# Batch 0 folded in two load halves, third-stage angles first among the tables, first-stage copies shared with the vector engine, and the products of an accumulating bank moved: a Fourier-mixing plus MLP-mixer kernel

## Chip, cores, metric

The kernel runs on one core of one Trainium2 chip. The metric is device time in microseconds (us); the 36 runs of the kernel before that are on record lie between 602.35 and 606.16. Engines in the profile: PE is the matrix engine (PEld its weight loads), DVE the vector engine, ACT the scalar engine, POOL (GpSimd) the general one, which also asks for most loads here.

## The reference, cut to what matters

```python
X = np.fft.fft(np.fft.fft(x, axis=1), axis=2).real       # x: 8 x 3008 x 256, float32
h = np.maximum(X.transpose(0, 2, 1) @ w_tok1, 0) @ w_tok2          # tokens, width 256
u = X + h.transpose(0, 2, 1)
out = u + np.maximum(u @ w_ch1, 0) @ w_ch2                         # channels, width 1536
```

The kernel computes in 16-bit floats and takes the Fourier transforms as products with tables of cosines and sines, which it makes itself while the first batch loads.

## The kernel before, where the change and the argument touch it

A batch goes through a *front*: its token rows are loaded twice (`xp` forwards, `xm` by a gather of backward rows with indices `ix8`), folded into even and odd parts `eo` and `pad`, multiplied by the first-stage table (`z`), then by the feature table `td` (`w`), then by the third-stage tables `tp` and `tq` (`yt`); the token MLP follows (`uu`, `ut`). Then come six *chunks* of channel MLP per batch: `pc` is the first layer, `pa` and `pb` hold the second. For most chunks the second layer uses seven products instead of eight, with sums `s` of the activations and weight sums `t1w` to `t4w`. The front of a later batch is woven into the chunks of the one before; the front of batch 0 stands alone at the start, where nothing can hide it.

The loads and the first tables (`ts`, `tt` and `stt` issue to DVE unless `eng=G`; `act` to ACT; `gdma` and `gather` are asked for by GpSimd):

```python
    new_x(0)
    load_xp(0)                                   # whole rows of batch 0
    iota(kb[:]...); iota(krow[:]...); iota(jrow[:]...)     # GpSimd
    ...
    ts(rowi[:], rowi[:], -2.0, AT.mult)
    ts(ix8[:], ix8f[:], rowi[:], AT.add, 0.0, AT.max)      # 128 x 16, one SBUF input
    load_xm(0, 0)
    load_xm(0, 1)
    ...
    load_w1p(); load_w1m()                       # first token weights, turned by tables
    ...                                          # later:
    def load_rest():
        load_wc1(0)                              # first channel weights, first half
        ...                                      # w2n, second token weights
        load_wc1(1)                              # first channel weights, second half
        gdma(wc2[:, :, 0:D], ...)                # second channel weights
```

The fold, the turns of the third-stage table, and the first stage (generators; each `yield` is a place where the caller may put other work between):

```python
        for t0, t1 in ((9, 17), (1, 9)) if b == 0 else ...:      # in fold(b, eng)
            tt(fa[:], xp[:, t, 1:128], rv[:, :, 255:128:-1], AT.add, eng)   # rv: rows of xm
            yield
            tt(fb[:], rv[:, :, 1:128], xp[:, t, 255:128:-1], AT.add, eng)
            ...
    def back(k, sgn):                            # turned tables for the token weights
        for c in range(3):
            ...
            nc.tensor.matmul(pr[:], lhsT=anti[:], rhs=tts[k][:, c4], start=True, stop=True)
            if k:
                act(tts[k + 1][:, c4], pr[:], scale=sgn)         # back(2): ACT
            else:
                V.tensor_copy(out=tts[k + 1][:, c4], in_=pr[:])  # back(0): DVE
            yield
        ...
        for t0 in (11, 6, 1):                    # in front(b): first stage
            for half in range(2):
                ...                              # ten products (b == 0) into pz
                copy(half == 0 and b > 0, zo[:, :, :, t0:t0 + 5], ...)   # True: DVE, else ACT
                yield
```

The order of batch 0's front, and the placing of the seven products in the chunks:

```python
    filler(12)                                   # products without use: keep the clock up
    take(fold0, 5)
    ...                                          # four small operations on the table td
    take(fold0, 5)
    own = front(0)
    take(tu_q, 3); take(tu_p, 2); take(own, 2); take(tu_r, 3)
    filler(4)
    take(own, 2); take(tu_b0, 2); take(own, 4); take(tu_b0, 1)
    new_x(1); load_xp(1)                         # loads of batch 1
    for k in range(2):
        load_xm(1, k)
    for k in range(6):                           # second stage, with the token weights turned
        take(own, 2)
        take(tu_b2, 1 if 0 < k < 4 else 0)
        take(car, 1)
    ...
    sum_at = {0: 1, 1: 2, 3: 4, 4: 3}            # column tile: sum s to make
    places = {0: 0, 1: -1, 2: 1, 4: 2, 6: 3, 7: 4, 9: 5, 11: 6}   # column tile: product
                # 0, 2, 4, 5 add into the bank pa; 1, 3, 6 are the bank pb; -1 only reads pa
```

After the first chunk product, GpSimd runs `weight_sums()` (two copies and four operations of about 1.5 us each) and DVE starts the fold of batch 1.

## Time and profile before

| | before |
|---|---|
| time, median of 2 | 603.07 us (602.35 to 603.78) |
| span of the profiled execution | 600.3 us |
| PE busy | 583.2 us (97%) |
| last write of `z` ends (first stage done) | 20.14 us |
| first chunk product `pc` starts | 33.92 us |
| first chunk product of batch 1 starts | 108.89 us |

PE is full nearly everywhere after 76 us, so the time is the length of PE's program plus what PE waits for. The list of waits of PE in the first 80 us of the kernel before (what was waited for, us in total, times, longest) names what is to be had:

```profile
PE filler L399 <- DVE ident L84: 8.8, 1, 8.8
PE pz L476 <- DVE eo L90: 1.0, 1, 1.0
PE pr L416 <- ACT tp L97: 0.6, 1, 0.6
PE pu L566 <- DVE ut L90: 0.4, 1, 0.4
PE pw L508 <- ACT z L97: 0.4, 1, 0.4
...
```

In the whole execution, one more line says that `pa` products waited 0.6 us for `s`. The timeline of DVE in the kernel before (start, us, line, operation, out<-in, shapes; in brackets the idle time before and who ended it):

```profile
1.87 1.72 DVE L86 TENSOR_SCALAR ix<-ix8f,rowi 128x16 int32<-128x16 f32 x1
...
10.37 0.71 DVE L90 TENSOR_TENSOR fa<-xp,xm 96x1016 f16<-96x1016 f16 x1
...
13.73 0.72 DVE L90 TENSOR_TENSOR fa<-xp,xm 96x1016 f16<-96x1016 f16 x1
...
17.88 1.29 DVE L439 CAST tts<-pr 128x512 f16<-128x512 f32 x2 [0.78 <-PE pr L435]
19.56 0.58 DVE L101 CAST z<-pz 128x96 f16<-128x96 f32 x1 [0.39 <-PE pz L476]
...
42.20 1.76 DVE L90 TENSOR_TENSOR fb<-xm,xp 96x508 f16<-96x508 f16 x1
```

Some short operations are long: 1.72 us for 16 elements, and 1.76 us for the last line. Between 16 and 20 us DVE has idle time: it makes only one of the eight copies of `z`.

The table of stretches of the kernel before (stretch, length, busy us of PE, PEld, DVE, ACT, POOL with counts, granted PE clock, DMA share, GB/s) shows the loads at about 200 GB/s from the start:

```profile
4.00:6.00 2.00, 0.00 (x0) 0.00 (x0) 1.72 (x12) 0.76 (x1) 1.52 (x3) 1.00 1.01 200
6.00:8.00 2.00, 0.00 (x0) 0.00 (x0) 1.87 (x12) 1.97 (x6) 1.92 (x4) 1.00 1.02 207
8.00:10.00 2.00, 1.20 (x12) 1.20 (x13) 1.50 (x7) 1.96 (x5) 1.92 (x5) 1.00 1.08 213
20.00:25.00 5.00, 4.75 (x49) 3.83 (x50) 3.90 (x10) 4.45 (x12) 3.32 (x5) 1.00 1.10 220
25.00:29.00 4.00, 3.93 (x44) 3.42 (x42) 3.09 (x7) 2.78 (x6) 0.96 (x1) 1.00 1.00 197
```

The clock column reads 1.00 also where no change of the clock is on record yet. The first record here is at 13.46 us, full from then on; before it the products ran at half rate (the 128-column fillers start 0.107 us apart near 9 us, products of that size 0.056 us apart after 14.3 us).

### The profile page before, as it was taken

What the parts mean: (1) busy time and instruction counts of PE and PEld (TensorE: products, weight loads), DVE (VectorE), ACT (ScalarE), POOL (GpSimd) and SP (SyncE); (2) the same over time, 40 slices, a digit from 0 to 9 for tenths busy, and PEclk for the clock granted to TensorE, in tenths of its full rate; (3) what the DMA queues carried; (4) which work ended last, traced back from release to release, by engine and by line L of the source; (5) the groups of instructions that cost most, each with busy time, mean ns of one, the idle gap of its engine ahead of it and who ended that gap; (6) DMA issues with size and microseconds to landing.
All of it is one profiled execution on the core that took longest, in us unless ns stands there. A gap on an engine that the chain in (4) does not pass through costs nothing.

```text
span 600.3 us, 15332 instructions
## 1 busy us (share of the span) xinstructions
PE 583.2 (97%) x6273; PEld 417.3 (70%) x6273; DVE 452.8 (75%) x924; ACT 387.3 (65%) x753; POOL 259.3 (43%) x396
## 2 busy tenths in 40 slices
PE   3899999999999999999999999999999999999997
PEld 3756676677767776667767777667767777666775
DVE  8779879686898668765898678856689757866663
ACT  8854665477647866577656866568665776546662
POOL 8650555937565554527348354565555100000000
PEclk9999999999999999999999999999999999999999
DMA  8993912275138914393335942278123422233533
GB/s 160 209 178 71 177 40 55 65 141 121 37 72 127 143 37 68 79 180 54 72 60 119 129 87 54 67 145 115 37 55 84 93 55 55 64 74 76 94 72 88
DMA packets 83414, 55.69 MB, mean 93 GB/s; under 512 B 53778, under 2 KB 80082, under 8 KB 82578
## 3 DMA queue, kind: packets, MB, share of 16 engines
q1 hardware_dynamic: 76816, 36.82, 32.2%
q0 software_dynamic: 6208, 17.63, 16.3%
q8 instruction: 49, 0.80, 0.6%
q10 hardware_dynamic: 320, 0.26, 0.2%
q14 instruction: 21, 0.17, 0.1%
HBM read 35.26 MB, written 24.64 MB: 100 GB/s over the span
## 4 chain that ended last, share of the span: by engine, by line
PE 81%; DVE 1%; issue 0%; ACT 0%; DVEq 0%
PE pc L662 35%; PE pa L712 17%; PE pb L712 13%; PE pu L566 5%; PE po L775 4%; PE pt L595 3%; PE pz L471 1%; PE py L538 1%; DVE s L90 1%; PE pw L508 1%; PE pw L512 1%; DVE osb L90 0%; DVE q L90 0%; DVE ut L90 0%; ACT c L97 0%
## 5 line engine op out<-in xcount | busy, mean ns | idle before, releaser
L97 ACT ACTIVATE c<-pc 128x512 f16<-128x512 f32 (+1 forms) x553 | 312.7, 591 | 159.9 <-PE pc L662 138.8
L662 PE MATMUL pc<-ut,wc 128*128 128x512 f16 (+1 forms) x1152 | 312.4, 374 | 0.4 <-DMA wc<-in_moe_w_ch_dram 0.3
L712 PEld LDWEIGHTS <-s 128*128 128x128 f16 x1968 | 122.8, 98 | 40.1 <-DVE s L90 5.7
L662 PEld LDWEIGHTS <-wc 128*128 128x128 f16 x1152 | 98.0, 98 | 55.7 <-issue 3.0
L712 PEld LDWEIGHTS <-c 128*128 128x128 f16 x1476 | 93.1, 97 | 27.8
L90 DVE TENSOR_TENSOR s<-c 128x1536 f16<-128x1536 f16 x82 | 82.0, 1000 | 4.7 <-ACT c L97 4.7
L90 DVE TENSOR_TENSOR q<-pa,uT 128x256 f32<-128x256 f32 x123 | 52.3, 425 | 36.3 <-PE pa L712 35.8
L908 POOL COPY hold<-s 128x1 f16<-128x1 f16 x29 | 5.4, 187 | 171.5 <-DVE s L90 171.5
L90 DVE TENSOR_TENSOR osb<-pb,q 128x256 f32<-128x256 f32 x123 | 51.9, 422 | 31.1 <-PE pb L712 28.4
L90 DVE TENSOR_TENSOR ut<-pu,yt 128x512 f16<-128x512 f32 (+1 forms) x96 | 63.0, 670 | 1.6 <-PE pu L566 1.5
L90 POOL TENSOR_TENSOR eo<-sab 96x512 f16<-96x512 f16 x48 | 53.9, 1139 | 1.6
L566 PE MATMUL pu<-w2r,uu 128*128 128x512 f16 (+1 forms) x168 | 50.0, 379 | 0.0
L90 POOL TENSOR_TENSOR sab<-fa,fb 96x256 f16<-96x256 f16 (+1 forms) x72 | 46.7, 673 | 0.0
L90 DVE TENSOR_TENSOR s<-s,c 128x1536 f16<-128x1536 f16 x41 | 41.1, 1003 | 0.0
L90 DVE TENSOR_TENSOR s<-c,s 128x1536 f16<-128x1536 f16 x41 | 39.5, 964 | 0.0
L97 ACT ACTIVATE w<-pw 128x257 f16<-128x257 f32 x90 | 34.6, 384 | 6.4 <-PE pw L512 3.6
L90 DVE TENSOR_TENSOR osb<-pa,uT 128x256 f32<-128x256 f32 x41 | 17.4, 424 | 24.8 <-PE pa L712 24.7
L775 PE MATMUL po<-wc,c 128*128 128x256 f16 x288 | 35.4, 273 | 0.0
L712 PE MATMUL pa<-t2w,s 128*128 128x128 f16 x492 | 34.2, 219 | 0.5 <-DVE s L90 0.4
L712 PE MATMUL pa<-t3w,s 128*128 128x128 f16 x492 | 34.2, 219 | 0.3 <-DVE s L90 0.2
L712 PE MATMUL pb<-wc,c 128*128 128x128 f16 x492 | 34.4, 219 | 0.0
L712 PE MATMUL pa<-wc,c 128*128 128x128 f16 x492 | 34.4, 219 | 0.0
(187 smaller groups left out, 747.8 us busy)
## 6 DMA issues: line engine op xcount, KB each, us to landing
out_dram<-osb SPq DMA_DIRECT2D x83, 256.0 KB
xp<-in_x_dram POOLq DMA_DIRECT2D x14, 408.0 KB, 6.6
out_dram<-osb SPq DMA_DIRECT2D x11, 192.0 KB
uT<-ut SPq DMA_TRANSPOSE x96
w2n<-in_moe_w_tok_dram POOLq DMA_DIRECT2D x2, 752.0 KB, 9.3
w1p<-in_moe_w_tok_dram POOLq DMA_DIRECT2D x2, 384.0 KB, 8.0
wc<-in_moe_w_ch_dram POOLq DMA_DIRECT2D x1, 768.0 KB, 14.7
xp<-in_x_dram POOLq DMA_DIRECT2D x2, 272.0 KB, 6.0
```

Of the source, the lines that this page charges most:

```text
L90: eng.tensor_tensor(out=out_, in0=a, in1=b, op=op)
L97: nc.scalar.activation(out=out_, in_=in_, func=func, scale=scale, **kw)
L471: nc.tensor.matmul(out_, lhsT=rows[:, half * P:half * P + P], rhs=tab, start=True, stop=True)
L508: nc.tensor.matmul(pw[:, 0:256].rearrange("p (h d) -> p h d", h=2)[:, :, 0:65], lhsT=zg[:, 0, g], rhs=td[:, 0:130].rearrange("p (h d) -> p ...
L512: nc.tensor.matmul(pw[:, 64:322].rearrange("p (h d) -> p h d", h=2)[:, :, 0:64], lhsT=zg[:, 1, g], rhs=td[:, 130:258].rearrange("p (h d) - ...
L538: nc.tensor.matmul(py[:, P * k:P * k + P], lhsT=w[:, 4 * c + k, o:o + P], rhs=tab[:, 4 * c + k, :], start=True, stop=True)
L566: nc.tensor.matmul(pu[:, 0:64 * nk], lhsT=uu[:, th, h, :], rhs=w2[:, th, :, 8 * c:8 * c + nk], start=(th == 0), stop=(th == 1))
L595: nc.tensor.matmul(pt[:, o:o + n], lhsT=hw[:, g, c], rhs=w[:, g, w0:w0 + n], start=(g == 0), stop=(g == NG - 1))
L662: nc.tensor.matmul(pc[:, 0:n], lhsT=wc1[:, h, ct * P:(ct + 1) * P], rhs=ut[:, c, h, 0:n], start=(h == 0), stop=(h == 1))
L712: nc.tensor.matmul(dst[:, P * a:P * a + P], lhsT=left[:, k, a, :], rhs=right[:, k, :], start=(first and k + a == 0), stop=(k == NH - 1), s ...
L775: nc.tensor.matmul(po[:, o:o + D], lhsT=c1[:, ct, ks * P:ks * P + P], rhs=wc2[:, ct, 0:D], start=(ct == 0), stop=(ct == NCT - 1))
L908: G.tensor_copy(out=hold[:], in_=pbox[3][:, 0, 0, 0:1])
```

## The change

The intent: shorten the 8.8 us before PE's first work and the stage after it. The upper token rows of batch 0 (9 to 16) are asked for alone, with the gather that belongs to them, so that the first fold needs fewer bytes. `ix8` becomes an operation with two SBUF inputs. The table `tp` is to be ready ahead of all others, so its turns go first, and the rest of the tables is made between the folds. DVE takes four copies of `z` and the three of `back(2)`, and gives the three of `back(0)` to ACT. All of `back(2)` and `turn_q` change places around the second stage. Last, three of the products of the chunks move one column tile later, so that their sums are ready. The diff, cut:

```diff
-    load_xp(0)
-    iota(kb...) ; iota(krow...) ; iota(jrow...)
+    load_xp(0, 9, NR)
 ...
-    ts(ix8[:], ix8f[:], rowi[:], AT.add, 0.0, AT.max)
+    stt(ix8..., ix8f..., rowi[:], zero[:], AT.add, AT.max)
     load_xm(0, 0)
+    iota(kb...) ; iota(krow...) ; iota(jrow...) ; iota(q2...)
+    load_xp(0, 0, 9)
     load_xm(0, 1)
 ... # masks from GpSimd to DVE; ident and lrot ahead of rest(m3); t1n, t1b, td into tables()
-                act(tts[k + 1][:, c4], pr[:], scale=sgn)
+                ts(tts[k + 1][:, c4], pr[:], sgn, AT.mult)
             else:
-                V.tensor_copy(out=tts[k + 1][:, c4], in_=pr[:])
+                act(tts[k + 1][:, c4], pr[:])
 ...
-                copy(half == 0 and b > 0, zo[:, :, :, t0:t0 + 5],
+                copy(half == 0 if b else t0 < 11, zo[:, :, :, t0:t0 + 5],
 ...
-    filler(12) ; take(fold0, 5) ; <td> ; take(fold0, 5) ; take(tu_q, 3) ; take(tu_p, 2)
-    take(own, 2) ; take(tu_r, 3) ; filler(4) ; take(own, 2) ; take(tu_b0, 2)
-    take(own, 4) ; take(tu_b0, 1)
+    filler(6) ; take(tu_p, 2) ; take(fold0, 3) ; take(tab, 1) ; take(fold0, 2)
+    take(own, 2) ; take(tu_r, 3) ; take(fold0, 2) ; take(tab, 1) ; take(fold0, 2)
+    take(tu_b0, 3) ; take(own, 2) ; take(tab, 1) ; take(fold0, 1) ; take(own, 2)
+    take(tu_b2, 3) ; take(own, 2)
     new_x(1) ; <loads of batch 1>
     for k in range(6):
         take(own, 2)
-        take(tu_b2, 1 if 0 < k < 4 else 0)
         take(car, 1)
+    take(tu_q, 3)
 ...
-    places = {0: 0, 1: -1, 2: 1, 4: 2, 6: 3, 7: 4, 9: 5, 11: 6}
+    places = {0: 0, 1: -1, 2: 1, 5: 2, 6: 3, 8: 4, 10: 5, 11: 6}
```

More of the change, by code (lines that the diff above doesn't have):

```diff
@@ L120, in new_x, with load_xp @@
                       xin.tile([KR, NR - 1, D], FP16, tag="xm", name="xm"))
-    def load_xp(b):
+    def load_xp(b, t0=0, t1=NR):
         xp = x_tiles[b][0]
@@ L127, in load_xp @@
                 p0 = i * QP + q
-                gdma(xp[p0:p0 + n, :, :],
-                     dram(x_t, (b * S + 16 * i + 64 * r) * D,
-                          [[64 * D, n], [1, NR * D]]))
+                gdma(xp[p0:p0 + n, t0:t1, :],
+                     dram(x_t, (b * S + 16 * i + 64 * r + t0) * D,
+                          [[64 * D, n], [1, (t1 - t0) * D]]))
     def load_xm(b, k):
@@ L157 @@
     w1m = stage.tile([P, NG, DTOK], FP16, tag="w1m")
-    tw23, q25 = pvec("tw23"), pvec("q25")
+    tw23 = pvec("tw23")
     def load_w1p():
@@ L173, in load_w1m @@
              dram(w1_t, 44 * DTOK, [[NQ * DTOK, 64], [1, 3 * DTOK]]))
+    zero = gen.tile([P, 2 * BB], FP32, tag="zero")
+    V.memset(zero[:], 0.0)
     V.memset(tw23[:], TWO23)
-    V.memset(q25[:], 0.25)
     V.memset(offrow[:, 0:2, :], 0.25)
@@ L179 @@
     iota(pcol[:], [[0, 1]], 0, 1)
-    iota(q2[:], [[1, 2]], -64, 1)
     iota(ix8f[:], [[376, BB], [1, 2]], 374, 0)
     new_x(0)
-    load_xp(0)
-    iota(kb[:].rearrange("p (c g k) -> p c g k", c=3, g=4), [[8, 3], [1, 4], [47, 64]], 0, 0)
-    iota(krow[:].rearrange("p (c g i) -> p c g i", c=3, g=4), [[8, 3], [1, 4], [4, 2]], 0, 0)
-    iota(jrow[:], [[1, 129]], 0, 0)
+    load_xp(0, 9, NR)
     ts(xicol[:], pcol[:], float(QP), AT.is_ge)
@@ L191 @@
     ts(rowi[:], rowi[:], -2.0, AT.mult)
-    ts(ix8[:], ix8f[:], rowi[:], AT.add, 0.0, AT.max)
+    stt(ix8[:].rearrange("p b k -> p (b k)"), ix8f[:].rearrange("p b k -> p (b k)"), rowi[:],
+        zero[:], AT.add, AT.max)
     load_xm(0, 0)
+    iota(kb[:].rearrange("p (c g k) -> p c g k", c=3, g=4), [[8, 3], [1, 4], [47, 64]], 0, 0)
+    iota(krow[:].rearrange("p (c g i) -> p c g i", c=3, g=4), [[8, 3], [1, 4], [4, 2]], 0, 0)
+    iota(jrow[:], [[1, 129]], 0, 0)
+    iota(q2[:], [[1, 2]], -64, 1)
+    load_xp(0, 0, 9)
     load_xm(0, 1)
@@ L200 @@
     load_w1p()
-    ts(mask[:, 0:1], pcol[:], float(NQ), AT.is_lt, eng=G)
-    ts(top[:], pcol[:], float(KR - 1), AT.is_lt, eng=G)
-    tt(mask[:, 1:2], xicol[:], top[:], AT.mult, eng=G)
     load_w1m()
@@ L228 @@
             pcol[h, :].unsqueeze(2).to_broadcast([64, NG, 64]), scale=0.0)
-    q47 = pvec("q47")
     scol, ge1, ge32, ge33, reff, offp, tgt, sgn = (
@@ L248 @@
     whole(v3[:], m3[:])
+    t1n = const.tile([KR, 2, 2, 24], FP16, tag="t1n")
+    t1b = const.tile([KR, 3, 24], FP16, tag="t1b")
+    t1m = stage.tile([KR, 96], FP16, tag="t1m")
+    t1c = stage.tile([KR, 72], FP16, tag="t1c")
+    ident, anti, lrot = (const.tile([P, P], FP16, tag=n, name=n)
+                         for n in ("ident", "anti", "lrot"))
     m1 = gen.tile([P, 5, 24], FP32, tag="m1")
@@ L253 @@
     cs = gen.tile([P, 5, 24], FP32, tag="cs")
+    q47 = pvec("q47")
     ts(q47[:], qcol[:], 1.0 / 47, AT.mult)
@@ L259 @@
     sin(cs[:], m1[:])
+    ts(ident[:], jrow[:, 0:P], pcol[:], AT.is_equal)
+    ts(ge1[:], scol[:], 1.0, AT.is_ge)
+    tt(tgt[:], ge1[:], ge32[:], AT.subtract)
+    tt(tgt[:], tgt[:], ge33[:], AT.subtract)
+    stt(tgt[:], tgt[:], 32.0, pcol[:])
+    ts(sgn[:], ge33[:], -2.0, AT.mult, 1.0, AT.add)
+    ts(lrot[:], jrow[:, 0:P], tgt[:], AT.is_equal, sgn[:], AT.mult)
     md = gen.tile([P, 257], FP32, tag="md")
@@ L275 @@
             act(md[:, o:o + n], jrow[:, 0:n], scale=d[:, k:k + 1], func=AFT.Identity, bias=off)
-    whole(vd[:], md[:])
-    ident, anti, lrot = (const.tile([P, P], FP16, tag=n, name=n)
-                         for n in ("ident", "anti", "lrot"))
-    ts(ge1[:], scol[:], 1.0, AT.is_ge)
-    tt(tgt[:], ge1[:], ge32[:], AT.subtract)
-    tt(tgt[:], tgt[:], ge33[:], AT.subtract)
-    stt(tgt[:], tgt[:], 32.0, pcol[:])
-    ts(sgn[:], ge33[:], -2.0, AT.mult, 1.0, AT.add)
+    ts(mask[:, 0:1], pcol[:], float(NQ), AT.is_lt)
+    ts(top[:], pcol[:], float(KR - 1), AT.is_lt)
+    tt(mask[:, 1:2], xicol[:], top[:], AT.mult)
     rest(m3[:], v3[:], m3[:])
@@ L288, with tables @@
         sin(tp[h, :, h], m3[h, :].rearrange("p (g k) -> p g k", g=NG))
-    ts(lrot[:], jrow[:, 0:P], tgt[:], AT.is_equal, sgn[:], AT.mult)
-    ts(ident[:], jrow[:, 0:P], pcol[:], AT.is_equal)
-    t1n = const.tile([KR, 2, 2, 24], FP16, tag="t1n")
-    t1b = const.tile([KR, 3, 24], FP16, tag="t1b")
-    t1m = stage.tile([KR, 96], FP16, tag="t1m")
-    t1c = stage.tile([KR, 72], FP16, tag="t1c")
-    rest(md[:], vd[:], md[:])
-    csv = cs[0:KR, 0:4, :].rearrange("p (a b) k -> p a b k", a=2)
-    for i in range(2):
-        ts(t1n[:, :, i, :], csv[:, :, i, :], mask[0:KR, i:i + 1], AT.mult)
-    ts(t1b[:, 1, :], cs[0:KR, 4, :], float(np.sqrt(0.5)), AT.mult,
-       mask[0:KR, 1:2], AT.mult)
-    V.tensor_copy(out=t1b[:, 0:3:2, :], in_=t1n[:, :, 0, :])
-    ts(t1m[:], t1n[:].rearrange("p a b k -> p (a b k)"), -1.0, AT.mult)
-    ts(t1c[:], t1b[:].rearrange("p a k -> p (a k)"), -1.0, AT.mult)
-    sin(td[:, 0:65], md[:, 0:65])
-    sin(td[:, 66:258], md[:, 65:257])
+    whole(vd[:], md[:])
+    def tables():
+        csv = cs[0:KR, 0:4, :].rearrange("p (a b) k -> p a b k", a=2)
+        for i in range(2):
+            ts(t1n[:, :, i, :], csv[:, :, i, :], mask[0:KR, i:i + 1], AT.mult)
+        ts(t1m[:], t1n[:].rearrange("p a b k -> p (a b k)"), -1.0, AT.mult)
+        yield
+        rest(md[:], vd[:], md[:])
+        sin(td[:, 0:65], md[:, 0:65])
+        sin(td[:, 66:258], md[:, 65:257])
+        yield
+        ts(t1b[:, 1, :], cs[0:KR, 4, :], float(np.sqrt(0.5)), AT.mult,
+           mask[0:KR, 1:2], AT.mult)
+        V.tensor_copy(out=t1b[:, 0:3:2, :], in_=t1n[:, :, 0, :])
+        ts(t1c[:], t1b[:].rearrange("p a k -> p (a k)"), -1.0, AT.mult)
+        ts(ol[:, 0:1], ol[:, 0:1], 2.0, AT.mult)
+        ts(td[:, 0:1], td[:, 64:65], 0.5, AT.mult, ol[:, 0:1], AT.add)
+        ts(td[:, 65:66], td[:, 64:65], 0.5, AT.mult, ol[:, 0:1], AT.subtract)
+        V.memset(td[:, 64:65], 0.0)
+        yield
     ts(acol[:], pcol[:], -1.0, AT.mult, 127.0, AT.add, eng=G)
@@ L814 @@
     fold0 = fold(0, V)
-    filler(12)
-    take(fold0, 5)
-    ts(ol[:, 0:1], ol[:, 0:1], 2.0, AT.mult)
-    ts(td[:, 0:1], td[:, 64:65], 0.5, AT.mult, ol[:, 0:1], AT.add)
-    ts(td[:, 65:66], td[:, 64:65], 0.5, AT.mult, ol[:, 0:1], AT.subtract)
-    V.memset(td[:, 64:65], 0.0)
-    take(fold0, 5)
     own = front(0)
-    take(tu_q, 3)
+    tab = tables()
+    filler(6)
     take(tu_p, 2)
+    take(fold0, 3)
+    take(tab, 1)
+    take(fold0, 2)
     take(own, 2)
     take(tu_r, 3)
-    filler(4)
+    take(fold0, 2)
+    take(tab, 1)
+    take(fold0, 2)
+    take(tu_b0, 3)
     take(own, 2)
-    take(tu_b0, 2)
-    take(own, 4)
-    take(tu_b0, 1)
+    take(tab, 1)
+    take(fold0, 1)
+    take(own, 2)
+    take(tu_b2, 3)
+    take(own, 2)
     new_x(1)
```

## The prediction

> **What bounds it now.** The page gives PE 97% busy. From 76 us on the table of stretches shows PE full nearly everywhere, so the tail of the kernel is TensorE work in program order. Idle PE is in the first 76 us: the list of waits puts 8.8 us before the first filler (DVE `ident`), 1.0 us on fold rows `eo`, 0.6 on `tp`, 0.4 on `z`; later 0.6 on the sums `s`, 0.4 on `ut`, 0.3 on `pad`.
>
> **What the change touches, from the timeline.**
> 1. The `ix8` operation took 1.72 us (1.87 to 3.58) for 16 elements beside GpSimd's DMA issue and `kb` iota. The Trainium skill, "SBUF — State Buffer" (the shared port pair, an exclusive lock), says that a DVE perf-mode operation and a GpSimd one block each other; this trace agrees. As the two-input form I expect about 0.2 us. The first gather then is issued at about 2.8 instead of 4.18 us.
> 2. `xp` landed at 8.24, the first half of `xm` at 9.82, the second at 11.86; the DMA moves about 0.205 MB/us. The first fold will need 0.79 MB, not 1.23: landed by about 8 us. It started at 10.37, behind DVE table work; now behind `rest(m3)`, about 9.0. Gain about 1.3 us.
> 3. The third-stage angles `tp` hardly gain: `kb` comes later on GpSimd, and identity, rotation and masks (about 0.9 us) now stand before `rest(m3)`. `tp` ready near 10.8, as before.
> 4. Against this, DVE gets four first-stage copies of `z` (0.6 us each) and the three of back(2) before `z` is whole, giving back(0) to ACT. Adding durations: two folds 5.5, tables 1.8, pads 0.5, copies 4.9, from 9.0: 21.8 us without a wait, likelier 22 to 23 because `anti` is ready only near 15.7. Before, the first `pw` started at 20.15. So the second stage starts 1.5 to 3 us later, but then without back(2) among its products: ACT and DVE waits there (about 1 us) go. Net by the `prot` product (25.56 before): 0 to 2.5 us later.
> 5. Fillers fall from 16 to 6 and a PE idle stretch follows: some matmuls may run at half rate for longer (512 columns were 0.43 us apart near 11 us, 0.22 later).
>
> **How much is on the path.** DMA is busy without a break from 4 to 42 us and moves the same bytes, so `xm` of batch 1 still lands near 41.4. DVE waited 1.8 us for it, then for the port until 43.9 (one 0.41 us operation took 1.76), and is then full until 62, where PE waits for its `pad`. A faster start is therefore lost there; a slower start is partly absorbed (about 1.2 us of PE waits between 52 and 72). The startup nets -0.3 to +1.3 us.
>
> **Moved products.** Those of `pa` go one column tile later, after their sums. Start-to-start gaps show excess waits of 0.18, 0.30, 0.32 and 0.56 us before t2w/t3w products: about 1.3 us in all, of which I expect 1 us back. The other chunks wait for nothing, so nothing more.
>
> **Prediction.** 602.3 us; 8 in 10 within 600.2 to 604.4. Faster by over 2%: 0.01, within: 0.98, slower: 0.01.
>
> **Right if** the first fold begins near 9 us; the first `pw` product comes after 20.2; batch 1's `xm` still lands at 41 to 42; DVE is full from 44 to 62; waits of PE for `s` fall under 0.3 us. **Wrong if** `z` is whole before 20 and batch 1 lands earlier (then 600 or less), if PE turns slow again before the second stage (another 1 to 2 us), or if the later `pa` products hold up the next chunk's first product: 0.1 us in each of 41 chunks would cost 4 us.

## The result, and the profile after

| | before | after |
|---|---|---|
| time, median of 2 | 603.07 us | 608.87 us (608.32 to 609.42) |
| PE's first work (filler) | 8.80 | 7.77 |
| `tp` done | 10.79 | 10.93 |
| first fold starts | 10.37 | 9.90 |
| second fold starts | 13.73 | 15.29 |
| `z` whole | 20.14 | 25.40 |
| `prot` product (second stage done) | 25.56 | 32.18 |
| first chunk product `pc` | 33.92 | 40.94 (+7.0) |
| first `pc` of batch 1 | 108.89 | 115.63 (+6.7) |
| last `pc` of all | 590.08 | 595.95 (+5.9) |

The kernel became 5.8 us slower: ratio 1.0096, 95% interval 1.0076 to 1.0116. A ratio is the mean time of one kernel's runs over that of the other's of the same rounds, so it is not quite the ratio of the medians quoted. The milestones say where: 7 us were lost before the first chunk, almost none of it (0.3 us) was won back in the chunks of batch 0, and about 0.9 us in all later ones.

The list of waits of PE, first 80 us, of the kernel after:

```profile
PE filler L410 <- DVE dr L86: 7.8, 1, 7.8
PE pt L419 <- ACT tp L97: 2.4, 1, 2.4
PE pw L523 <- DVE z L101: 2.1, 1, 2.1
PE pz L487 <- DVE eo L90: 0.9, 2, 0.6
PE pz L507 <- DVE pad L90: 0.9, 2, 0.6
PE pz L507 <- ACT z L97: 0.7, 1, 0.7
...
```

No line for `s` is left in the whole execution: the moved products wait no more. New are the 2.1 us before the second stage, and gaps for `pad` and `z` just before it. The timeline of DVE after:

```profile
1.88 0.24 DVE L93 SCALAR_TENSOR_TENSOR ix<-ix8f,rowi,zero 128x16 int32<-128x16 f32 x1
...
9.90 0.69 DVE L90 TENSOR_TENSOR fa<-xp,xm 96x1016 f16<-96x1016 f16 x1 [0.54 <-DMA xm<-in_x_dram,ix]
...
15.29 0.69 DVE L90 TENSOR_TENSOR fa<-xp,xm 96x1016 f16<-96x1016 f16 x1 [1.96 <-DMA xm<-in_x_dram,ix]
...
19.02 1.48 DVE L101 CAST z<-pz 128x480 f16<-128x480 f32 x2 [0.65 <-PE pz L487]
...
21.50 0.49 DVE L90 TENSOR_TENSOR pad<-xp 96x64 f16<-96x64 f16 x4
21.91 1.21 DVE L101 CAST z<-pz 128x480 f16<-128x480 f32 x2
23.04 1.87 DVE L84 TENSOR_SCALAR tts<-pr 128x512 f16<-128x512 f32 x3
24.83 0.57 DVE L101 CAST z<-pz 128x96 f16<-128x96 f32 x1
```

`ix8` is short, as intended. But the second half of the rows comes late (1.96 us of waiting), and from 19 us on DVE works through a queue without a gap: copies, tables, `pad`, copies, the three copies of `back(2)`, and only then the last copy of `z`, for which PE stands. The timeline of PE after shows it standing:

```profile
23.16 0.22 PE L519 MATMUL pw<-td,z 128*128 128x130 f16 x1
25.45 0.29 PE L523 MATMUL pw<-td,z 128*128 128x128 f16 x1 [2.08 <-DVE z L101]
```

The table of stretches after, for the same stretches:

```profile
4.00:6.00 2.00, 0.00 (x0) 0.00 (x0) 0.79 (x4) 1.13 (x2) 2.00 (x6) 1.00 1.03 168
6.00:8.00 2.00, 0.23 (x3) 0.33 (x4) 1.85 (x15) 1.18 (x3) 1.69 (x3) 1.00 1.03 164
8.00:10.00 2.00, 0.57 (x6) 0.31 (x3) 1.36 (x7) 1.95 (x5) 2.00 (x4) 1.00 0.84 116
20.00:25.00 5.00, 2.08 (x26) 1.19 (x24) 4.82 (x19) 0.60 (x1) 3.07 (x4) 1.00 1.13 217
25.00:29.00 4.00, 3.54 (x25) 2.96 (x26) 2.11 (x5) 1.64 (x4) 2.10 (x4) 0.57 1.03 212
```

Three readings. The loads moved 116 to 168 GB/s where before they moved 200 to 213. From 20 to 25 us DVE is full (4.82 of 5.00) and ACT empty (0.60), where before they were 3.90 and 4.45. And right after, the clock is 0.57: the record has PE at half rate from 25.22 to 28.64 us, a stretch of 3.41 us. From 28.64 us on it is full again.

So there are four suspects for the loss: the slower loads, the copies on DVE, the half-rate stretch, and the new order of turns and tables.

### The profile page after: what moved, and what is told of

It reads as the page before. It is cut to its first block, busy times and chain, and to the rows that moved or that the text cites. A ratio compares the mean times of both kernels' runs of the same rounds, so it can differ in the third digit from the quotient of the medians.

```text
span 606.2 us, 15315 instructions
## 1 busy us (share of the span) xinstructions
PE 585.4 (97%) x6263; PEld 419.5 (69%) x6263; DVE 453.6 (75%) x931; ACT 388.6 (64%) x749; POOL 259.2 (43%) x395
## 4 chain that ended last, share of the span: by engine, by line
PE 81%; DVE 1%; issue 0%; DVEq 0%
PE pc L673 35%; PE pa L723 17%; PE pb L723 13%; PE pu L577 6%; PE po L786 4%; PE pt L606 3%; PE pz L482 1%; PE py L549 1%; PE pw L523 1%; PE pw L519 1%; DVE s L90 1%; DVE osb L90 0%; DVE ut L90 0%; PE pz L507 0%; DVE q L90 0%
## 5 line engine op out<-in xcount | busy, mean ns | idle before, releaser
L673 PE MATMUL pc<-ut,wc 128*128 128x512 f16 (+1 forms) x1152 | 316.5, 374 | 0.3 <-DVE ut L90 0.3
L90 POOL TENSOR_TENSOR sab<-fa,fb 96x256 f16<-96x256 f16 (+1 forms) x72 | 48.1, 693 | 0.0
L723 PE MATMUL pb<-b,s 128*128 128x128 f16 x492 | 34.2, 219 | 0.0
L723 PE MATMUL pb<-t1w,s 128*128 128x128 f16 x492 | 34.2, 219 | 0.0
```

The lines of the kernel that those rows point to most:

```text
L90: eng.tensor_tensor(out=out_, in0=a, in1=b, op=op)
L673: nc.tensor.matmul(pc[:, 0:n], lhsT=wc1[:, h, ct * P:(ct + 1) * P], rhs=ut[:, c, h, 0:n], start=(h == 0), stop=(h == 1))
L723: nc.tensor.matmul(dst[:, P * a:P * a + P], lhsT=left[:, k, a, :], rhs=right[:, k, :], start=(first and k + a == 0), stop=(k == NH - 1), s ...
```

## The experiments

Ratios are against the kernel before of the same rounds, with the 95% interval. "Pc" is the start of the first chunk product in the profile (33.92 before, 40.94 after).

### 1. The moved products alone

Edit, on before: only the line `places` is the new one.

> The kernel before with only the new places of the accumulating bank's products. Theory: the moved products take away four waits for the sums (0.2 to 0.6 us each) and change nothing else, so about -1.1 us (602.0), the first chunk's first product still near 33.9 us, and the span between the first chunk and the last shorter by 1.1 us. Rival: the products interact with the shifted start and are worth nothing alone: within 0.3 us of before.

Measured: 601.92 us against 603.61, ratio 0.9978 (0.9964 to 0.9991), so 1.3 us gained. The estimate was 1.0. The single runs are 601.79 to 601.92 and 603.29 to 603.74; the profile is of the slowest and is used in experiment 13. The products are a small gain, so the loss comes from the other parts of the change.

### 2. The split loads alone, in the old order

```diff
-    load_xp(0)
+    load_xp(0, 9, NR)
 ...
     load_xm(0, 0)
+    load_xp(0, 0, 9)
     load_xm(0, 1)
```

> The kernel before with only the token rows of batch 0 asked for in two halves (upper rows, first gather, lower rows, second gather), all else in place. Theory 1 (the split slows the loads): DMA rate falls to 100-170 GB/s between 5 and 12 us, the second gather lands near 14 to 15 us instead of 11.9, DVE waits for it 1 us or more, first chunk later by 1 to 2 us. Rival (the slow loads come from the moved index tables and DMA issue order, not from the split): rate stays over 195, second gather by 12.5, total unchanged within 0.5 us.

Measured: 605.5 us, ratio 1.0028 (1.0013 to 1.0044): 1.7 us lost. The table of stretches of this kernel:

```profile
4.00:6.00 2.00, 0.00 (x0) 0.00 (x0) 1.72 (x12) 0.75 (x1) 1.82 (x4) 1.00 0.77 133
6.00:8.00 2.00, 0.00 (x0) 0.00 (x0) 1.90 (x12) 1.97 (x6) 1.70 (x3) 1.00 0.92 131
```

It moved 133 GB/s instead of 200. The upper rows alone are too few bytes to keep the queue filled until the gather's bytes come: the gather was issued at 4.20 us, its first packet left at 5.92, and between 5.5 and 6.0 us on the mean 1.5 of the 16 DMA engines were busy. The later loads fell further behind (first token weights 17.07 against 15.73, last rows of batch 1 47.24 against 43.55), but only 0.7 us is in pc (34.61). The profiled execution was the slowest of the four (607.86): the fold of batch 1 began at 45.31 instead of 41.56, one of its operations took 1.76 us, PE waited 2.8 us for `ut` (two waits, to 54.40 and to 56.19), and from 55.42 to 62.25 it ran at half rate. The other three, without a profile, were 604.89 to 605.54. What made the rest of their 1.7 us is therefore not shown.

### 3. After, with the rows asked for whole

```diff
-    load_xp(0, 9, NR)
+    load_xp(0)
 ...
-    load_xp(0, 0, 9)
```

> The changed kernel with the token rows of batch 0 asked for whole again, all else as changed. Theory 1: DMA rate back over 195 GB/s, second gather lands by 12.5 us instead of 15.2, the wait of 1.96 us before the second fold goes, first chunk near 39 us and the total 1.5 to 2.5 us below the changed kernel. Rival: loads stay slow (issue order), total as changed.

Measured: 612.11 us, ratio 1.014 (1.0123 to 1.0156); pc at 43.44. The expectation missed: the repair made it worse. The loads did come in time (second fold at 13.80, no wait), but `z` was whole at 25.08, hardly earlier than the 25.40 of after. The DVE timeline shows why, and something new at 37 us:

```profile
16.55 0.42 DVE L90 TENSOR_TENSOR eo<-fb,fa 96x504 f16<-96x504 f16 x1
18.71 1.47 DVE L101 CAST z<-pz 128x480 f16<-128x480 f32 x2 [1.74 <-PE pz L486]
...
37.56 1.24 DVE L84 TENSOR_SCALAR uu<-uv 128x128 f16<-128x128 f32 x1
...
40.75 1.24 DVE L84 TENSOR_SCALAR uu<-uv 128x128 f16<-128x128 f32 x1
```

First, the wait for data only turned into a wait for products: in PE's order the second pair of `pz` stands behind the turned tables. These ran from 15.32 to 18.05 us at half rate, for the clock was full only from 18.12 us; no run has whole rows and an early full clock together, so how much of this wait the clock makes is open. Second, `uu` took 1.24 us. At that time GpSimd made its weight sums (timeline of POOL, same kernel):

```profile
37.22 1.51 POOL L90 TENSOR_TENSOR t1w<-wc 128x768 f16<-128x768 f16 x1
...
40.39 1.51 POOL L90 TENSOR_TENSOR t3w<-b,wc 128x768 f16<-128x768 f16 x1
```

The weights had landed, the sums ran ahead of the first chunk, and they met the token MLP of the late batch 0. PE waited 1.6 us for it, and was at half rate again from 42.01 to 45.42 us. The Trainium skill, "SBUF — State Buffer" (section "SBUF: two separate sides"), says that DVE and GpSimd share a port pair that is an exclusive lock: when DVE runs in a mode that uses two ports, or reads two SBUF inputs while GpSimd reads SBUF too, whichever starts first holds it for its whole instruction, and the other waits. The trace agrees: two `uu` operations of 1.24 us beside operations of 1.51 us. The list of waits names the DMA of `xm` for these 1.6 us of PE, which had nothing to do with it.

### 4. Experiment 3 with GpSimd held back

```diff
+    G.tensor_copy(out=hold[:], in_=uu0[0][:, 1, 1, 0:1])   # waits for uu, ahead of weight_sums()
```

> The slow variant with whole token rows (612.1), and GpSimd's sums of the second channel weights made to wait for the last token product's result (uu). Theory (DVE's uu and uv operations are shut out of the shared SBUF port while GpSimd adds weights): those DVE operations fall from 0.7 to 1.2 us to under 0.35 us, the wait of 1.8 us before the token-mixing products goes, first chunk 2.5 to 3.5 us earlier than 43.4. Later folds may then meet the weight sums instead. Rival (the wait has another cause, a load): first chunk stays at 43 us.

Measured: 607.83 us, ratio 1.0076 (1.0058 to 1.0094), pc at 40.97, so 2.5 us earlier than in experiment 3. DVE and POOL timelines of this kernel, in that order:

```profile
39.39 0.23 DVE L84 TENSOR_SCALAR uu<-uv 128x128 f16<-128x128 f32 x1
```

```profile
41.43 1.51 POOL L90 TENSOR_TENSOR t1w<-wc 128x768 f16<-128x768 f16 x1
```

Both `uu` operations are 0.23 us (the other at 37.97) once GpSimd works after them. So the collision is shown as the cause of what experiment 3 lost on top. It is not a cause in the kernel after, where the weights land later and the collision is smaller (PE waited 0.2 us for `uu`; 0.9 us in the execution of experiment 14). Without it, whole loads in the changed order bring little: 1.0076 against 1.0096 with overlapping intervals. In this profile PE was at half rate for two windows (23.80 to 30.62) and in that of after for one, which can hide a gain; experiment 7 has neither.

### 5. No gap between the asks

```diff
     load_xm(0, 0)
+    load_xp(0, 0, 9)
     iota(kb...) ; iota(krow...) ; iota(jrow...) ; iota(q2...)
-    load_xp(0, 0, 9)
```

> The changed kernel with the lower token rows asked for right after the first gather, ahead of GpSimd's index tables, so that two halves are kept but no issue gap is left. Theory (the loads starve in the gap between issues, the halves themselves cost nothing): DMA rate over 190 GB/s from 5 to 12 us and second gather landed by 13 us, but kb and so the third-stage angles 1 us later. Rival (half-rows are slow to move in themselves): rate still falls to 100-170 and the second gather lands near 15.

Measured: 611.34 us, ratio 1.0125 (1.0095 to 1.0155). The loads were repaired here too (second fold 13.78, about 200 GB/s from 7 us), `tp` was 1.2 us later (12.16) because `kb` was, `z` whole at 24.87, and `uu` met the weight sums (1.24 us, PE waited 1.8 us). This is experiment 3 again: in these runs, with the products before 16 to 18 us at half rate, earlier data did not make `z` earlier.

### 6. After, with the former engines for the copies

```diff
-                ts(tts[k + 1][:, c4], pr[:], sgn, AT.mult)
+                act(tts[k + 1][:, c4], pr[:], scale=sgn)
 ...
-                act(tts[k + 1][:, c4], pr[:])
+                V.tensor_copy(out=tts[k + 1][:, c4], in_=pr[:])
 ...
-                copy(half == 0 if b else t0 < 11, zo[:, :, :, t0:t0 + 5],
+                copy(half == 0 and b > 0, zo[:, :, :, t0:t0 + 5],
```

> The changed kernel with the copies of the first-stage and turned tables on the engines they had before (first-stage copies and the last turned tables on ACT, first turned tables on DVE). Theory 2 (DVE's program order holds back the first stage): z is whole 2 to 4 us earlier than 25.4, PE stays at full rate then, and the first chunk comes 3 to 5 us earlier than 40.9; total 604 to 606. Rival (late data alone): z whole within 1 us of 25.4, total within 1.5 us of the changed kernel.

Measured: 604.49 us, ratio 1.002 (1.0004 to 1.0035). `z` whole at 22.44, pc at 36.29, and no half-rate stretch after 16.92 us. ACT makes the last copy of `z` here:

```profile
21.82 0.62 ACT L97 ACTIVATE z<-pz 128x96 f16<-128x96 f32 x1
```

The copies are the largest part: 1.0096 less 1.0020 is 0.76% or 4.6 us.

### 7. Former copy engines and whole loads

The edits of experiments 3 and 6 together.

> The changed kernel with both the copies back on their former engines and the token rows asked for whole. Theory (the two parts that cost time are the DVE copies and the starved loads): second gather near 11.9 us, z whole by 21.0, first chunk by 35 us, total like the kernel with the moved products alone, 601.5 to 603. Rival (the new order of tables and turns costs as well): first chunk still 1.5 us or more later than in the kernel before, total 603.5 or more.

Measured: 604.15 us against 602.91, ratio 1.0028 (1.0006 to 1.0051); `z` whole at 22.71, pc at 36.57. Nothing gained over experiment 6. So undoing the split alone wins nothing in the changed order, with either set of engines (the clock was full from 17.57 us here, not from 13.46 as in the kernel before). Here ACT makes the copy of the `pad` half of `z`, and stands first behind its three copies of `back(2)` until 22.22 us: the same queue, on the other engine.

### 8. The copies alone, in the old order

The inverse edit of experiment 6, on before.

> The kernel before with the change's engines for the copies alone, its own order kept. Theory (the copies cost time only in the change's order, where DVE has to finish tables, pads and the last turned tables ahead of the last copy; in the old order DVE sat idle there): z whole within 0.5 us of 20.1, first chunk within 0.5 us, total within 1 us of before. Rival (DVE copies are dear in themselves): z 2 us or more later, total 2 to 4 us over before.

Measured: 603.36 us against 603.44, ratio 1.0005 (0.9975 to 1.0035); `z` whole at 20.54. The DVE timeline:

```profile
16.58 0.53 DVE L90 TENSOR_TENSOR pad<-xp 96x64 f16<-96x64 f16 x4
17.24 3.30 DVE L101 CAST z<-pz 128x480 f16<-128x480 f32 x5
```

The same copies, on the same engine, cost nothing that the time shows (the interval leaves -1.5 to +2.1 us) when they fall where DVE was idle: behind the folds, back to back, with no tables and no `back(2)` between. The profile is less kind: pc is at 34.87, 0.95 us later than before, so this part of the expectation was missed; 0.4 us of it came with `z`, and another 0.4 in the second stage, where `back(2)` now shares DVE with the copies of `w`. So most of the loss is neither the copies nor the order alone but both: the order puts 1.87 us of `back(2)` copies and the tables into the one queue that ends in `z`.

### 9. After, with the clock kept up

```diff
     take(tu_b2, 3)
+    filler(10)
     take(own, 2)
+    filler(36)
```

> The changed kernel with 46 more filler products in the idle PE time ahead of the second stage (10 after the turned tables, 36 before the second stage). Theory (3.4 us at half clock from 25.2 us cost about 1.6 us): no half-rate stretch in the trace after 18.4 us, first chunk at 39.2 to 39.8 instead of 40.9, total about 607.3. Rival (copies set the pace there, so the clock is worth nothing): first chunk within 0.4 us of 40.9.

Measured: 606.28 us, ratio 1.0052 (1.0036 to 1.0069), pc at 38.31, 2.6 us earlier than after. The table of stretches:

```profile
20.00:25.00 5.00, 4.18 (x67) 3.63 (x65) 4.53 (x16) 0.64 (x2) 3.75 (x6) 1.00 1.13 219
25.00:29.00 4.00, 4.00 (x45) 3.51 (x43) 3.43 (x9) 3.63 (x9) 1.42 (x2) 1.00 1.04 214
```

46 useless products during PE's waits removed the half-rate stretch, and with it 1.0096 less 1.0052, 0.44% or 2.7 us (each ratio is known to about 0.2%). A stretch of 3.41 us at half rate can cost half its length at most, 1.7 us. In the two profiles, 0.9 of the 2.6 us in pc came with `z` (24.52, because the rows landed earlier: second fold at 14.40 against 15.29), and 1.4 us between `z` and `prot`: 5.42 us here, as in the kernel before (5.42), and 6.78 at half rate. Experiment 14 shows that the stretch can also be two windows long. Since the half rate after 17 us is also gone in experiment 6, a good part of what the copies cost looks to be the price of the clock.

How idle must PE be? The Trainium skill, "TensorE: Matmul & The Clock Gate" ("Part 1: The HAM clock gate"), states a free-running window of 3413 ns, and a fall to half rate after at least one idle window. The stretches here, 3.41 and 6.83 us, agree with that window. But while the clock was full, no wait of PE in the kernel after was as long as a window: the longest was 2.08 us (the 2.4 us for `tp` lie before). Counted from the traces of all kernels, in windows on the grid of each run's own clock changes in the first 60 us: every window in which PE was busy 43% of the time or less was followed by half rate (six cases; 26% in the kernel after); every one with 67% or more stayed full; between 52% and 62%, four fell (among them the 59% of experiment 10 and 62% in the second kernel of experiment 11) and six did not. What decides among those, these runs don't show.

### 10. After, with `back(2)` in the second stage again

```diff
-    take(tu_b2, 3)
 ...
     for k in range(6):
         take(own, 2)
+        take(tu_b2, 1 if 0 < k < 4 else 0)
         take(car, 1)
```

> The changed kernel with only the last turned tables (back of 2) taken among the second stage's products again, as before. Theory (everything that stands on DVE ahead of the last first-stage copy delays the second stage by its own time): z whole 1.8 us earlier than in the changed kernel (near 23.6), first chunk 1 to 2.5 us earlier than 40.9 (more if PE stays warm), total 606.5 to 608. Rival: the DVE copies of the turned tables only move the wait, total as changed.

Measured: 609.06 us against 603.77, ratio 1.0086 (1.0055 to 1.0117). `z` was whole 2.2 us earlier (23.22), as the queue says it should be (1.6 us against the execution of experiment 14, whose second fold began at 14.71, here 14.42), but nothing came of it: pc at 41.51. The table of stretches for the time after:

```profile
20.90:27.70 6.80, 5.54 (x38) 3.97 (x39) 4.79 (x12) 2.24 (x5) 3.77 (x6) 0.50 1.10 219
```

Without those products PE idled more ahead of the second stage, the clock fell two windows instead of one, and `uu` met the weight sums (PE waited 0.9 us for it). The same two occur in the execution of experiment 14. The expectation was a miss. It shows that one milestone is not the time: what PE does while it waits counts too.

### 11. Former copies and `back(2)` late; and the same kept warm

The first kernel has the edits of experiments 6 and 10 together. The second adds this, to see if the first one's slow clock until 18.92 us mattered:

```diff
-    filler(6)
+    filler(30)
```

> The changed kernel with the copies on their former engines and the last turned tables among the second stage again; split loads, order of tables and moved products stay. Theory: nothing but the colder PE and the split is left, z whole near 20.9 to 21.4, first chunk near 35, total 602 to 603, within 1 us of the kernel with the moved products alone. Rival (the order of tables itself costs): z whole after 22, total over 603.5.

Measured: 605.63 us, ratio 1.0032 (1.0007 to 1.0056); `z` whole at 21.86, pc at 36.55, no better than experiment 6. The products of `tq` and their waits now stand in the second stage, which takes what `z` gains.

> The changed kernel with former copy engines and the late last turn (605.6 in the last run, first chunk at 36.6), and 30 filler products at the start instead of 6, so that TensorE is busy up to the third-stage angles. Theory (what is left of the loss is the first stage at half rate, up to 17 to 19 us in these kernels and 13.5 in the kernel before): full rate from 13 us or earlier, first chunk 0.8 to 1.8 us earlier, total 603.5 to 605. Rival (order of tables and turns): first chunk within 0.4 us of 36.6.

Measured: 605.8 us against 603.44, ratio 1.0034 (1.0009 to 1.006). The clock was full from 13.67 us and `z` was whole at 21.86 exactly as in the first kernel: in this order and with split loads, the slow clock at the start cost nothing. But PE then waited for `pad` and `anti` and fell to half rate for two windows, 20.50 to 27.32, so pc was 38.74.

### 12. After, warm everywhere

`filler(30)` at the start and the fillers of experiment 9.

> The changed kernel with fillers in both idle stretches of TensorE (30 at the start, 10 and 36 ahead of the second stage). Theory: the late fillers are worth 2.6 us as in the earlier run, the early ones little, because there DVE is late in any case: first chunk at 37.5 to 38.4, total 605.5 to 606.3 against 603.0 to 603.8 for the kernel before. Rival: the early clock matters by itself, first chunk under 37.3.

Measured: 606.05 us, ratio 1.0044 (1.0014 to 1.0074), pc at 38.49: as experiment 9 within the intervals. So more fillers at the start bring nothing back. They did not make the clock full earlier either (16.79 us, against 16.09 in experiment 9), so this run does not test the early clock; the waits before the second stage are what the other fillers filled.

### 13. A better version

In the profile of experiment 1 the fold of batch 1 met the weight sums, and PE waited 1.8 us for `ut` later (DVE and POOL timelines, then the waits between 40 and 80 us):

```profile
44.57 1.76 DVE L90 TENSOR_TENSOR fb<-xm,xp 96x508 f16<-96x508 f16 x1
```

```profile
44.33 1.72 POOL L90 TENSOR_TENSOR t4w<-wc,t2w 128x768 f16<-128x768 f16 x1
```

```profile
PE pc L662 <- DVE ut L90: 1.8, 2, 1.4
...
```

The last sum `t4w` waits for the second channel weights, the last of the constant loads. On top of experiment 1 they are asked for earlier:

```diff
         for th in range(2):
             gdma(w2n[:, th, :], ...)
-        load_wc1(1)
         gdma(wc2[:, :, 0:D], ...)
+        load_wc1(1)
```

> The kernel before with the moved products, and the second channel weights asked for ahead of the second half of the first ones. Theory (batch 1's first fold is held up by GpSimd's weight sums on the shared port, which start when those weights land): sums start about 2 us earlier, the fold operation that took 1.76 us takes 0.41 us, PE waits near 52 to 55 us fall by 0.5 us or more; total 601.0 to 601.5 against 603, with less scatter than the moved products alone (601.8 to 603.7). Rival (the loads of batch 1 alone set it): total as with the moved products alone.

Measured: 601.33 us (601.00 to 601.51) against 603.77, ratio 0.9958 (0.9937 to 0.9978). This beats both kernels: by 2.4 us the one before in the same rounds, and by 7.5 us the median quoted for the one after. DVE and POOL timelines of this kernel:

```profile
42.18 0.41 DVE L90 TENSOR_TENSOR fb<-xm,xp 96x508 f16<-96x508 f16 x1
```

```profile
39.98 1.54 POOL L90 TENSOR_TENSOR t4w<-wc,t2w 128x768 f16<-128x768 f16 x1
```

The sums end at 41.5 us, before the fold of batch 1 begins at 41.84; `fb` takes 0.41 us, and the waits of 1.8 us are gone (0.4 us for `ut` is left, as in the kernel before). The five runs lie within 0.5 us, where experiment 1 had two groups 1.5 us apart. The two kernels were not in the same rounds, so their difference (0.9978 to 0.9958) is inside the intervals; the profile shows its mechanism.

The last one adds the two-input `ix8` to it:

> As the last one, with the gather's row numbers made by the two-input form as in the change, nothing else of its start. Theory (this operation was shut out of the port by GpSimd's work): it takes 0.24 instead of 1.7 us, third-stage angles done near 9.5 instead of 10.8 us, first fold then waits for the loads, first chunk 0.3 to 1 us earlier; but the loads of batch 1 land as before, so the total gains less than 0.5 us. Rival (a faster start is kept): total 0.5 to 1 us under the last one.

Measured: 601.32 us, ratio 0.9963 (0.9942 to 0.9983): no change. `tp` was ready at 9.40 instead of 10.04, but then the first fold waited for its rows until 10.21 (10.01 without), and pc was 33.87 (33.52 without). So no faster start came about; whether one would be lost later, as the prediction had argued, this run does not test.

### 14. The kernel after, once more

> The changed kernel itself, as a control on the same chip: total 1.0096 times before within 0.002; second gather lands 14 to 15.5 us, z whole 24.5 to 25.5, a half-rate stretch in the second stage, first chunk 40 to 42.

Measured: 608.56 us (607.57 to 612.41) against 603.44, ratio 1.0095 (1.0048 to 1.0142): the result stands. In this execution the second fold waited 2.25 us, `z` was whole at 24.83, and the half rate lasted two windows (22.57 to 29.40), so where the clock falls varies from run to run.

## Why the prediction was right or wrong

The predicted 602.3 us, with 600.2 to 604.4, was wrong: it became 608.87. That it stays within 2% was right.

**Right.** `ix8` fell from 1.72 to 0.24 us, as the shared lock led to expect. `tp` was done at 10.93 (10.8 predicted). The moved products brought 1.3 us in experiment 1 and no wait for `s` is left. That the fold of batch 1 is held by the port is right too, and experiment 13 makes a gain of it.

**The step that failed** is "The startup nets -0.3 to +1.3 us". It was +7.0 us at the first chunk product. Four terms of that sum were wrong.

1. `z` whole at *"likelier 22 to 23"* was 25.40. The sum of DVE durations (21.8) was taken from 9.0 without waits. The first fold began at 9.90, because its gather, asked for 1.2 us earlier than before, landed at 9.78 (9.82 before). The lower rows landed at 15.16 (11.86 before): DMA moved 116 to 168 GB/s, because they were asked for only at 5.32 us, behind the index tables; without that gap it moved 192 to 198 from 6 us on (experiment 5). Yet with the rows in time (experiments 3 to 5) `z` was whole at 25.08, 24.54 and 24.87, and with split loads (experiments 9, 12 and 14) at 24.52, 24.69 and 24.83. In these runs what binds is the chain of DVE and PE in the new order, in which the last copy of `z` stands behind tables, `pad`, and 1.87 us of copies for `back(2)`. The prediction listed these durations but not who stands behind whom.
2. *"Some matmuls may run at half rate for longer"* stood in the argument for the first idle stretch, where it cost nothing in the one order that tests it (second kernel of experiment 11). A slow turn before the second stage was listed only among what would make the prediction wrong, at 1 to 2 us, and had no place in the sum. It came there; the fillers that removed it gave 2.7 us (experiment 9), and in the profiles it took 1.4 us between `z` and `prot`.
3. *"A slower start is partly absorbed (about 1.2 us of PE waits [...])"* was 0.3 us: +7.02 at the first chunk and +6.74 at batch 1. The waits taken for slack, 0.26 us for `pad` and 0.42 us for `ut`, are in both traces with the same length: they come from what stands just before them, and move along with a delay. And `xm` of batch 1 did not land at 41.4 but at 43.54, and DVE was not full from 44 to 62: it idled 3.5 us near 50 us.
4. *"ACT and DVE waits there (about 1 us) go"*, so that `prot` would be 0 to 2.5 us later: it was 6.6 us later, of which 5.3 us had come with `z`. Nothing of that 1 us came: with the clock full, the time from `z` to `prot` was 5.42 and 5.43 us (experiments 9 and 12), as before (5.42).

**The sum, by parts.** Moved products: -1.3 us (experiment 1). The copies on DVE in this order: +4.6 us (after against experiment 6); fillers alone recover 2.7 us (experiment 9), so the half rate is in these 4.6 us and not beside them. The rest, from experiment 1 (0.9978) to experiment 6 (1.0020), is 0.42% or 2.5 us; it belongs to the new order of loads, tables and turns. Summed, -1.3 + 4.6 + 2.5 = 5.8 us, which closes by construction, since the parts are differences along one row of ratios, each known to about 0.2% (1 us). That the copies cost nothing measurable in the old order (experiment 8) shows that the parts are not independent.

**Open.** Which of the table order, the turn order and the split loads makes the 2.5 us is not settled. The split loads cost 1.7 us in the old order (experiment 2) but nothing could be won back by undoing them in the new one (experiment 7), so the 1.7 us cannot simply be taken out of it. `back(2)` among the second stage's products, as before, brings nothing either (experiment 11, first kernel). A rival stays untested: in the kernels with the new order and the rows in time the clock became full at 16.15 to 18.12 us, in the kernel before at 13.46.

## What to carry to other kernels

Before moving work to an idle engine, write down its queue in program order and ask what the *last* operation that the bottleneck waits for stands behind; the sum of durations is right only if nothing in that queue waits. When the bottleneck engine will idle in pieces, count the price of its clock, also at the stage after the idle pieces. A gap that has the same length in two traces at different times is a local dependency and absorbs no delay; and when a load is made earlier, ask which work of GpSimd it releases and what that meets on the shared port.

## What the Trainium skill lacked or had wrong

- "TensorE: Matmul & The Clock Gate", "Why this matters for your kernels", asks to avoid idle gaps over about 3 us. Here PE fell to half rate with no gap over 2.1 us, in several pieces: after windows of 3.41 us that were busy 26% in the kernel after, and up to 62% in others. The page does tell, under "A second HAM failure mode: psum-queue depth-cycling", of a kernel whose frequent short idles made the clock swing, but a share of busy time (here 43% or less always fell, 67% or more never, between them both) is not on it.
- "DMA: Bandwidth & Descriptors", "Latency and other measured facts", gives about 1 us to the first byte of a load that GpSimd asks for. Here it was 1.4 us from issue to first packet for the first load (1.38 to 2.79 us in the kernel after) and 1.7 us for a gather (4.20 to 5.92 in experiment 2), and what matters for a start is that the bytes asked for before must cover this time: with too few, 133 GB/s instead of 200 in experiment 2.
- "SBUF — State Buffer", "SBUF: two separate sides", has the exclusive lock, and the trace agrees (0.23 against 1.24 us for `uu`, 0.41 against 1.76 us for `fb`). It doesn't say how the lock looks in a profile: the blocked operation is drawn long, on both engines (`t4w` 1.72 us against 1.54), and PE's wait of 1.6 us behind it was put down to a DMA.
